# Pooled attention and top-1 experts on one core: two of eight folds keep three chunks, the token numbers are cast by ScalarE, and the order is made anew

## The chip, the core and the metric

The kernel runs on one core of a Trainium2 chip. TensorE (PE) multiplies, VectorE (DVE), ScalarE (ACT) and GpSimd (POOL) work on elements, SyncE (SP) issues most DMAs; each engine works through a queue of its own, in a fixed order, and waits on semaphores. The metric is the time of one execution in microseconds of the device.

## The reference

For 8 batches, 8 heads, 1152 positions and head size 64: queries are averaged in pairs (576 pooled queries), then softmax attention over all 1152 keys. Its output, as 4608 tokens of 512 features, goes through a layer of 8 experts of which each token takes the best one.

```python
q_pool = q.reshape(B, H, S // 2, 2, D).mean(axis=3)
scores = np.matmul(q_pool, k.transpose(0, 1, 3, 2)) / np.sqrt(D)
attn = np.exp(scores - scores.max(-1, keepdims=True))
attn = attn / (attn.sum(-1, keepdims=True) + 1e-09)
x = np.matmul(attn, v)                       # then as (4608, 512)
logits = x @ w_gate
expert_idx = np.argmax(logits, axis=1)       # gate_w: softmax value of it
for e in range(E):
    mask = expert_idx == e
    out[mask] = gate_w[mask, None] * (np.maximum(x[mask] @ w1[e], 0.0) @ w2[e])
```

## The kernel before

Attention goes batch by batch, pair of heads by pair (four), and half of the queries by half (288 columns): a unit. A unit's scores come in nine chunks of 128 keys. For each chunk TensorE makes the scores of both heads in four tiles of 64 x 64 (L592) into one of two banks `st`, and VectorE takes them to SBUF as `s` while it keeps a running minimum (L597). The minimum of all chunks goes over TensorE (L615) and VectorE (L621) to `bias`; ScalarE takes exponentials of three chunks at a time (L625); TensorE multiplies them with the values (L696), and ScalarE and VectorE add the two halves of that into `xT` (L701, L702). Four units may be in flight (`s` has four buffers).

The sums of the exponentials: POOL folds the nine chunks of a unit to one in three adds (L671 to L674): chunks 0 to 2 plus 3 to 5, plus 6 to 8, and then, of the three chunks that are left, the third onto the first. TensorE sums what is left over the partitions, in four tiles of 32 columns (L680). So `total` reads chunk 0 and chunk 1 of `fold`. The last three pairs of the last batch are not folded: TensorE sums all nine chunks (L666).

Keys and pooled queries are transposed by TensorE in two pieces for each pair (L537, L543) and copied out by ScalarE to `kT` and `qT` (L549, L559): one piece with key chunk 8 and the queries, one with key chunks 0 to 7. POOL makes the pooled queries (L496).

At the end of a batch comes its routing. The sums are turned and inverted to `rec` (L711 to L724). TensorE makes the logits (L771), ScalarE copies them (L792), TensorE turns them (L778), and VectorE works out the expert, the gate and the place of each token in its expert's list (L784 to L838): `weight` holds the cast of the token numbers `tok` to integers (L824), `count` adds 576 to `tok` for the next batch (L838). ScalarE copies `rec` in twelve small pieces (L854), VectorE transposes rows (L859), SP writes them to DRAM, and POOL writes the lists with six indirect DMAs (L875).

The experts follow: POOL gathers rows by indirect DMA (L976), ScalarE and VectorE split tokens and weights in a high and a low part (L1144, L1161, L1099), TensorE multiplies three times for each product (L1193, L1224, L1254), POOL scatters the results (L1262).

The order is not written out by hand. A planner (class `Flow`, method `emit`) takes steps with an engine, an expected duration, a key, predecessors and buffers, and works through a plan in which each free engine takes the ready step with the lowest key whose buffers are free. Constants named K_... set the keys of load, transposes, maximum, exponentials, folds, values and routing against their unit; KEEP says how far in key TensorE may stay in one tiling. What comes out is the fixed order of every engine's queue. Buffers and semaphores follow from that order.

Of the kernel before, what the change touches and what calls it, by code (L numbers as in the profile page):

```python
# [12 lines left out]
I32 = mybir.dt.int32  # L13
# [12 lines left out]
COLS, QUADS, ROWS = 1, 2, 3  # L26
# [1 line left out]
FOLD_BUFS = 2  # L28
ROW_BUFS = 3
PAIR = 40  # L30
K_LOAD = -57
K_V = -36
K_POOL = -7
K_PIECE = -26
K_TOP = -17
K_MAX = -18
K_EXP = 13
K_SUM = 25
K_AV = 51
K_ROW = 47  # L40
K_ROUTE = 55
K_CHAIN = 0
K_FIRST = 37
K_PUT = 88
K_SPREAD = 4
K_NEXT = 41
TABLE_OPS = 3
REST = (32, 64)
K_TAB = 0
K_SLOT = 45  # L50
SLOT = 100
RAW = 6
XT = 2
LI_BUFS = 6
RE_BUFS = 8
LEAD = 100
AHEAD = 270
XR2 = 4
XR = 7
Y_BUFS = 3  # L60
DMA = 2000
KEEP = 21
LAST = 3
EXPS = 3
FILL = 3
# [3 lines left out]
CALM, CALM_X = 700, 500  # L69
# [23 lines left out]
class Flow:  # L93
# [8 lines left out]
    def add(self, eng, ns, fn, key=0.0, after=(), holds=(), tiled=False, late=0, paced=0):  # L102
        if self.room is None:
            fn()
            return None
        for h in holds:
            h.left += 1
        step = [key, len(self.steps), eng, ns, fn, list(holds), 0, [], True, list(after), tiled, late, paced]
        for a in after:
            a[7].append(step)  # L110
            step[6] += 1
        self.steps.append(step)
        return step
# [154 lines left out]
def kernel(  # L268
# [10 lines left out]
    nc = tc.nc  # L279

    B, H, S, D = q.shape
# [5 lines left out]
    NJ = NQ // QP  # L287
    HQ = NQ // 2
    NC = S // P
    NHP = H // 2  # L290
# [3 lines left out]
    NQD = P // BL  # L294
# [32 lines left out]
    ones4 = const.tile([P, NHP, 2, 32], F32, name="ones4")  # L327
# [62 lines left out]
    tok = const.tile([QP, NJ], F32, name="tok")  # L390
# [25 lines left out]
    class Pools:  # L416
        h = None
# [29 lines left out]
    def pool(n):  # L447
        return 138 + 2.137 * n
# [14 lines left out]
    def done(*steps):  # L463
        return [s for s in steps if s is not None]
# [190 lines left out]
    def chunk_sum(o, f, key, s, ready, b, hp, half, sums, last):  # L655


        key += K_SUM
        if not o.exact and b == B - 1 and hp >= NHP - LAST:

            def whole():
                for i in range(0, NC, 2):
                    for j in range(min(2, NC - i)):
                        for h in range(2):
                            to = slice(64 * j + 32 * h, 64 * j + 32 * h + 32)
                            nc.tensor.matmul(sums.t[to, :HQ], ones4[:, hp, half, :], s.t[:, i + j, h], start=False,  # L666
                                             stop=hp == NHP - 1 and half == 1 and i + j + 2 >= NC, tile_position=(0, to.start))

            return f.add("PE", 485 * (NC + 1) // 2, whole, key + 10, [*every(ready), *done(*last)], [s, sums], COLS)
        u = tile_of(o, "fold", [P, 3, 2, HQ], bufs=FOLD_BUFS, pool=o.rt)  # L670
        add = lambda to, a, b: nc.gpsimd.tensor_tensor(to, a, b, ALU.add)  # L671
        p = f.add("POOL", pool(6 * HQ), lambda: add(u.t, s.t[:, 0:3], s.t[:, 3:6]), key, every(ready[:6]), [s, u])
        p = f.add("POOL", pool(6 * HQ), lambda: add(u.t, u.t, s.t[:, 6:9]), key, done(p, *every(ready[6:])), [s, u])
        p = f.add("POOL", pool(2 * HQ), lambda: add(u.t[:, 0], u.t[:, 0], u.t[:, 2]), key, done(p), [u])  # L674

        def total():
            for i in range(2):
                for h in range(2):
                    to = slice(64 * i + 32 * h, 64 * i + 32 * h + 32)
                    nc.tensor.matmul(sums.t[to, :HQ], ones4[:, hp, half, :], u.t[:, i, h], start=hp == half == 0,  # L680
                                     stop=hp == NHP - 1 and half == 1, tile_position=(0, to.start))

        return f.add("PE", 500, total, key + 15, done(p, *last), [u, sums], COLS)

    def values(o, f, key, x, s, ready, hp, half, xT):
        pa = [bank(o), bank(o)]
# [55 lines left out]
    def routing(o, f, key, b, xT, rec, sums, ready, hold=()):  # L742
# [5 lines left out]
        lw, ex, de = (tile_of(o, n, s, bufs=1) for n, s in (  # L748
            ("lw", [QP, NJ, H, NE]), ("ex", [QP, NJ, NE]), ("de", [QP, NJ, NE])))
        mx, fm, gate = (tile_of(o, n, [QP, NJ], bufs=1) for n in ("lmx", "fm", "gate"))  # L750
        ohb = tile_of(o, "ohb", [QP, NJ, NE], BF16, bufs=1)
        di = tile_of(o, "di", [QP, NJ], I32, bufs=one)
        re = tile_of(o, "re", [QP, NJ, 2], bufs=one)
        chain = [lw, ex, de]
        key -= (b == B - 1) * 20
        at = key + K_ROUTE
# [34 lines left out]
        p = f.add("PE", 1050, logits, at, ready, [pl, xT], COLS)  # L791
        p = f.add("ACT", act(HQ) - 44, lambda: nc.scalar.copy(lg.t, pl.t[:, :HQ]), at, done(p), [pl, lg])  # L792
        p = f.add("PE", 330, turn, at, done(p), [pt, lg])
# [25 lines left out]
        def weight():  # L819

            nc.vector.tensor_reduce(sum_(), ex.t, axis=AX.X, op=ALU.add)
            nc.vector.tensor_scalar(gate.t, sum_(), 1e-9, None, op0=ALU.add)

            nc.vector.tensor_copy(re.t.bitcast(I32)[:, :, 0], tok)  # L824
            nc.vector.reciprocal(re.t[:, :, 1], gate.t)

        def places():
# [11 lines left out]

        gap = K_CHAIN if b is not None and b < B - 2 else 0  # L840
        p = f.add("DVE", 1100, best, at + 2 + gap, done(*weighed), [*chain, pt])
        e = f.add("ACT", 230, lambda: nc.scalar.activation(ex.t, ex.t, AF.Exp), at + 2 + gap, done(p), [ex])
        p = f.add("DVE", 920, first, at + 2 + 2 * gap, done(p), [pt, ohb])
        r = f.add("PE", 360, rank, at + 3 + 2 * gap, done(p), [pr, ohb])
        w = f.add("DVE", 640, weight, at + 3 + 3 * gap, done(p, e), [ex, re, pt])
        p = f.add("DVE", 670, places, at + 3 + 4 * gap, done(r, w), [pr, pt, de, di])
        c = f.add("DVE", 400, count, at + 4 + 5 * gap, done(p), [pt, lw, ex, de])

        def put(g):

            row = tile_of(o, "row", [P, NJ, RUN], bufs=ROW_BUFS)

            def spread(d):
                nc.scalar.copy(row.t[d * BL:(d + 1) * BL, :, P:],  # L854
                               recf()[g * BL:(g + 1) * BL].rearrange("p j (a s) -> p j a s", s=2)[:, :, :, d * BL // D])

            def turn(j0):
                cols = xT.t.rearrange("p a (j g i) -> p j g a i", j=NJ, g=NB)
                nc.vector.transpose(row.t[:, j0:j0 + NR, :P].rearrange("p j (a x) -> p j a x", a=NHP), cols[:, j0:j0 + NR, g])  # L859

            def store():
                bq = b if b is not None else o.batch
                first = bq * NQ + g * BL * NJ
                rows = planes[:, first:first + BL * NJ] if isinstance(bq, int) else planes[:, bass.ds(first, BL * NJ)]
                for d in range(NQD):
                    nc.sync.dma_start(out=rows[d].rearrange("(i j) x -> i (j x)", j=NJ),
                                      in_=row.t[d * BL:(d + 1) * BL].rearrange("p j x -> p (j x)"))

            at = key + K_ROUTE + K_PUT * g / NB
            p = [f.add("ACT", 115, lambda d=d: spread(d), at + K_SPREAD, ready, [rec, row]) for d in range(NQD)]  # L870
            p += [f.add("DVE", dve(NR * P), lambda j=j: turn(j), at + K_PUT * j / NJ / NB, ready, [row, xT]) for j in range(0, NJ, NR)]
            return f.carry("SP", 480 * NQD, store, -1000.0, done(*p, *hold), [row], 1900)

        def enlist(j):
            ins = nc.gpsimd.indirect_dma_start(  # L875
                out=lists, out_offset=bass.IndirectOffsetOnAxis(ap=di.t[:, j:j + 1], axis=0),
                in_=re.t[:, j, :], in_offset=None, bounds_check=NE * LIST - 1, oob_is_err=False,
            )
            if b is not None:

                for other in stores:
                    tc.declare_no_dep(ins.ins, other.ins, reason="places in the lists are unique")
                stores.append(ins)
            return ins

        outs = [c]
        for g in range(NB):
            outs.append(put(g))
        for j in range(NJ):
            outs.append(f.carry("POOL", 1230, lambda j=j: enlist(j), at + (K_PUT if b is None or b < B - 2 else 0) * j / NJ, done(p, *hold), [di, re], 40, 4400, paced=CALM))  # L890
        return outs

    def first_slots(o, f, key, ready):
# [383 lines left out]
    with ExitStack() as cm, ExitStack() as units, ExitStack() as pairs:  # L1277
# [14 lines left out]
        hold = []  # L1292
# [8 lines left out]
        for b in range(B):  # L1301
            xT = tile_of(o, "xT", [P, NHP, NQ])
            rec = tile_of(o, "rec", [QP, 2, 3, H])
            sm = tile_of(o, "sm", [P, HQ], bufs=1)
            outs, sums, summed = [], sum_bank(o), []
# [6 lines left out]
            key = PAIR * (b * NHP + NHP)  # L1312
            outs.append(row_sums(o, f, key, sums, done(*summed), rec, sm, b == B - 1))
            outs = routing(o, f, key, b, xT, rec, sums, [*outs, router], hold)
            if b == B - 2:
                hold, first = first_slots(o, f, key + K_FIRST, outs)
# [9 lines left out]
        at = key + K_SLOT  # L1326
        for i, ns in enumerate(((EARLY_N,),) * EARLY + RANKS):
            s = i if i < EARLY else i - EARLY
            w, experts = Pools(), (early if i < EARLY else ranked)[:, 0]
# [20 lines left out]
    with tc.If(some > 0):  # L1350
        again = nc.values_load(stab[0:1, 1:2], min_val=0, max_val=1,
                               skip_runtime_bounds_check_because="a comparison's result")
        with tc.If(again > 0):
            reset_state()
            empty_lists()
            with ExitStack() as cm:
                o = open_attention(True, cm, cm, cm)
                with tc.For_i(0, B, 1) as b:
                    f = Flow()
                    xT = tile_of(o, "xT", [P, NHP, NQ])  # L1360
                    rec = tile_of(o, "rec", [QP, 2, 3, H])
# [52 lines left out]
```

## Time and profile before

| | us |
|---|---|
| median of 3 runs (1199.91 to 1202.28) | 1201.47 |
| the profiled execution | 1202.09 |
| its span | 1200.5 |
| TensorE busy | 1163.5 |
| POOL busy | 851.3 |
| VectorE busy | 785.4 |
| ScalarE busy | 636.6 |

The span runs from the first instruction to the end of the last. Attention ends at about 744 us, the experts fill the rest. The logits of the batches start at 121.26, 211.72, 298.80, 388.44, 480.05, 571.42, 660.68 and 750.34 us, and a stretch from one to the next is called a batch here. TensorE's granted clock is at its higher level, 2.4 GHz, in nearly the whole span (mean 0.995 of it). A busy TensorE is not one at its peak: products in different tiles overlap, so their pace is read from start to start.

### The profile page before, as it was taken

The numbers are of one execution on the slowest core, as the hardware profiler recorded it, in microseconds if no ns is written. First come the engines' busy times: TensorE is split into PE (matmuls) and PEld (weight loads), VectorE is DVE, ScalarE is ACT, GpSimd is POOL, SyncE is SP. The second block draws the span as 40 slices with busy tenths as digits, with TensorE's granted clock in tenths as the row PEclk, the third lists the DMA queues.
The fourth block names the chain that finished last, engine by engine and source line by source line (L and its number), as shares of the span: only waits on it lengthen the run. The fifth ranks groups of instructions, "written<-read, shape, count | busy, mean of one in ns | idle before, by whom it ended". The sixth has DMA issues, their size and how long they took to land.

```text
span 1200.5 us, 34022 instructions
## 1 busy us (share of the span) xinstructions
PE 1163.5 (97%) x14199; PEld 819.5 (68%) x14199; DVE 785.4 (65%) x2149; ACT 636.6 (53%) x786; POOL 851.3 (71%) x469
## 2 busy tenths in 40 slices
PE   8999999999999999999999999999999999999996
PEld 4555565555565455465556555898898989999985
DVE  5767867867867866876867965885454644536440
ACT  4666666666666566566666546443342433525440
POOL 2999899899899899899999625355666665541010
PEclk9999999999999999999999999999999999999999
DMA  6653435424624424635425432584353434525320
GB/s 178 147 147 94 109 64 138 108 65 111 134 63 121 100 70 112 128 68 131 111 68 133 89 121 86 139 240 135 93 162 89 154 118 128 152 89 186 120 84 20
DMA packets 78050, 138.12 MB, mean 115 GB/s; under 512 B 11321, under 2 KB 35777, under 8 KB 77888
## 3 DMA queue, kind: packets, MB, share of 16 engines
q1 hardware_dynamic: 68176, 116.22, 37.0%
q0 software_dynamic: 9712, 19.64, 5.6%
q8 instruction: 113, 1.85, 0.7%
q14 instruction: 49, 0.40, 0.1%
HBM read 115.04 MB, written 21.02 MB: 113 GB/s over the span
## 4 chain that ended last, share of the span: by engine, by line
PE 46%; issue 4%; POOL 3%; DVE 3%; ACT 2%; DMA 1%; POOLq 0%; DVEq 0%; ACTq 0%
PE ph L1193 16%; PE py L1254 11%; PE m L696 6%; PE st L592 5%; PE py L1224 5%; POOL fold L671 2%; PE sums L666 1%; DVE s L597 1%; ACT s L625 1%; PE sums L680 1%; DMA qn<-in_q_dram 1%; PE m L1243 0%; POOL xr L976 0%; POOL qp L496 0%; DVE row L859 0%
## 5 line engine op out<-in xcount | busy, mean ns | idle before, releaser
L597 DVE TENSOR_SCALAR_CACHE_REDUCE s<-st 128x576 f32<-128x576 f32 x576 | 419.5, 753 | 158.4 <-PE st L592 152.6
L625 ACT ACTIVATE s<-s,bias 128x1728 f32<-128x1728 f32 x192 | 320.5, 1729 | 166.8 <-DVE bias L621 151.9
L592 PE MATMUL st<-qT,kT 64*64 64x288 f32 x4608 | 364.3, 410 | 10.5 <-DVE s L597 8.6
L696 PE MATMUL m<-s,vn 64*64 64x288 f32 x4608 | 356.5, 405 | 0.0
L592 PEld LDWEIGHTS st<-qT,kT 64*64 64x64 f32 x4608 | 160.2, 132 | 150.3 <-DVE s L597 61.6
L696 PEld LDWEIGHTS m<-s,vn 64*64 64x64 f32 x4608 | 176.1, 133 | 85.9 <-issue 3.5
L671 POOL TENSOR_TENSOR fold<-fold,s 128x1728 f32<-128x1728 f32 x58 | 224.6, 3873 | 1.3
L671 POOL TENSOR_TENSOR fold<-s 128x1728 f32<-128x1728 f32 x58 | 224.3, 3868 | 1.2 <-ACT s L625 1.1
L976 POOL DMA_INDIRECT xr<-x_runs,ix x99 | 109.4, 1105 | 86.3 <-DMA raw<-in_moe_w_dram 20.7
L1193 PE MATMUL ph<-xh,w1h 128*128 128x384 f32 (+6 forms) x480 | 151.4, 315 | 4.0 <-ACT xh L1144 3.0
L1193 PE MATMUL ph<-xl,w1h 128*128 128x384 f32 (+6 forms) x480 | 149.7, 312 | 0.3 <-DVE xl L1099 0.3
L1193 PE MATMUL ph<-xh,w1l 128*128 128x384 f32 (+6 forms) x480 | 149.2, 311 | 0.0
L1262 POOL DMA_INDIRECT out_dram<-y,rec x41 | 45.6, 1112 | 143.0 <-ACT hh L1200 49.7
L1202 DVE SCALAR_TENSOR_TENSOR hl<-ph,hh 128x384 fp32r<-128x384 f32 (+5 forms) x100 | 54.9, 550 | 96.9 <-ACT hh L1200 82.6
L1200 ACT ACTIVATE hh<-ph 128x384 fp32r<-128x384 f32 (+5 forms) x100 | 48.7, 487 | 128.6 <-PE ph L1193 115.1
L1193 PEld LDWEIGHTS ph<-xh,w1h 128*128 128x128 f32 x480 | 91.2, 190 | 7.5 <-ACT xh L1144 3.5
L1193 PEld LDWEIGHTS ph<-xl,w1h 128*128 128x128 f32 x480 | 91.1, 190 | 1.6 <-DVE xl L1099 1.0
L1193 PEld LDWEIGHTS ph<-xh,w1l 128*128 128x128 f32 x480 | 90.9, 189 | 0.0
L1254 PE MATMUL py<-w2h,hh 128*128 128x512 f32 x224 | 88.6, 395 | 0.0
L1254 PE MATMUL py<-w2h,hl 128*128 128x512 f32 x224 | 88.3, 394 | 0.0
L1254 PE MATMUL py<-w2l,hh 128*128 128x512 f32 x224 | 88.0, 393 | 0.0
L875 POOL DMA_INDIRECT lists<-re,di x48 | 46.2, 963 | 55.9 <-PE m L696 21.4
(188 smaller groups left out, 1474.1 us busy)
## 6 DMA issues: line engine op xcount, KB each, us to landing
raw<-in_moe_w_dram SPq DMA_DIRECT2D x80, 512.0 KB
qn<-in_q_dram SPq DMA_DIRECT2D x62, 384.0 KB
vn<-in_v_dram SPq DMA_DIRECT2D x32, 576.0 KB
kn<-in_k_dram SPq DMA_DIRECT2D x31, 576.0 KB
x_runs<-row SPq DMA_DIRECT2D x96, 99.0 KB
xr<-x_runs,ix POOLq DMA_INDIRECT x99
x_runs<-empty SPq DMA_DIRECT2D x4, 297.0 KB
xq<-x_runs,ix POOLq DMA_INDIRECT x49
```

The lines of the kernel that those rows point to most:

```text
L592: made = nc.tensor.matmul(pt.t[to, h, :HQ], x.kT.t[up, c * P + i * D:c * P + (i + 1) * D], x.qT.t[up, cols], start=True, stop=True, tile_p ...
L597: nc.vector.tensor_scalar(s.t[:, c], pt.t[:, :, :HQ], -SCALE, None, op0=ALU.mult, op1=ALU.min, accum_out=mx.t[:, c:c + 1],)
L625: nc.scalar.activation(s.t[:, c0:c0 + n], s.t[:, c0:c0 + n], AF.Exp, bias=bias.t, scale=-1.0)
L671: add = lambda to, a, b: nc.gpsimd.tensor_tensor(to, a, b, ALU.add)
L696: made = nc.tensor.matmul(pa[i].t[cs, :HQ], x.vn.t[up, h, c, :], s.t[up, c, h], start=c == 0, stop=c == NC - 1, tile_position=(up.start, c ...
L875: ins = nc.gpsimd.indirect_dma_start(out=lists, out_offset=bass.IndirectOffsetOnAxis(ap=di.t[:, j:j + 1], axis=0), in_=re.t[:, j, :], in_o ...
L976: return nc.gpsimd.indirect_dma_start(out=x.xr[i // NQD].t[:, i % NQD, :], out_offset=None, in_=xg, in_offset=bass.IndirectOffsetOnAxis(ap ...
L1193: made = nc.tensor.matmul(view()[:, i, :], a[:, c, fp], b[:, c, :n], start=c == 0 and k == 0, stop=c == NDC - 1 and k == 2)
L1200: a = f.add("ACT", act(nb * n) - 44, lambda fs=fs, view=view: nc.scalar.activation(hidden(m)[0][:, fs, :n], view(), AF.Relu), at - 20, don ...
L1202: d = f.add("DVE", dve(nb * n), lambda fs=fs, view=view: nc.vector.scalar_tensor_tensor(hidden(m)[1][:, fs, :n], view(), 0.0, hidden(m)[0] ...
L1224: made = nc.tensor.matmul(py.t[:, :n], a[:, c % 2, ds], b[:, c, :n], start=c == 0 and k == 0, stop=c == NFC - 1 and k == 2)
L1254: made = nc.tensor.matmul(py.t[:n], a[:, c, hs], b[:, c % 2, :], start=c == 0 and k == 0, stop=c == NFC - 1 and k == 2)
```

## The change

Four things change. In the second half of every odd pair the third add is left out; TensorE sums the third chunk itself, two halves of 144 columns for two heads, in the four tiles. The cast of the token numbers moves from VectorE to ScalarE, as a step of its own that is ready when the routing begins; the writes of the lists and the add to `tok` wait for it. The planner expects 225 instead of 115 ns for each of the small copies of `rec` (and other figures for the steps above). And nearly all constants of the planner have other values, so the order of all engines is another from the first pair on.

```diff
-K_V = -36
-K_POOL = -7
-K_PIECE = -26
+K_V = -26
+K_POOL = -1
+K_PIECE = -12
...
-KEEP = 21
+KEEP = 12
...
-        p = f.add("POOL", pool(2 * HQ), lambda: add(u.t[:, 0], u.t[:, 0], u.t[:, 2]), key, done(p), [u])
+        three = hp % 2 and half
+        if not three:
+            p = f.add("POOL", pool(2 * HQ), lambda: add(u.t[:, 0], u.t[:, 0], u.t[:, 2]), key, done(p), [u])
...
+            for i in range(2 if three else 0):
+                for h in range(2):
+                    to = slice(64 * i + 32 * h, 64 * i + 32 * h + 32)
+                    w = slice(i * HQ // 2, (i + 1) * HQ // 2)
+                    nc.tensor.matmul(sums.t[to, w], ones4[:, hp, half, :], u.t[:, 2, h, w], start=False,
+                                     stop=last, tile_position=(0, to.start))
+
+        return f.add("PE", 750 if three else 500, total, key + 15, done(p, *last), [u, sums], COLS)
...
-            nc.vector.tensor_copy(re.t.bitcast(I32)[:, :, 0], tok)
...
-        w = f.add("DVE", 640, weight, at + 3 + 3 * gap, done(p, e), [ex, re, pt])
+        i = f.add("ACT", 200, lambda: nc.scalar.copy(re.t.bitcast(I32)[:, :, 0], tok), at, done(*ready), [re])
+        w = f.add("DVE", 460, weight, at + 3 + 3 * gap, done(p, e), [ex, re, pt])
...
-        c = f.add("DVE", 400, count, at + 4 + 5 * gap, done(p), [pt, lw, ex, de])
+        c = f.add("DVE", 400, count, at + 4 + 5 * gap, done(p, i), [pt, lw, ex, de])
...
-            p = [f.add("ACT", 115, lambda d=d: spread(d), at + K_SPREAD, ready, [rec, row]) for d in range(NQD)]
+            p = [f.add("ACT", 225, lambda d=d: spread(d), at + K_SPREAD, ready, [rec, row]) for d in range(NQD)]
```

How the queues change is seen in three places (numbers in names tell buffers apart; lines of the changed kernel are 9 higher behind the new products). TensorE before, in the second batch: values, three score products in a row, values, one score product, a fold's sums, transposed keys.

```order
L696 MATMUL m_1990<-s_1639,vn_1306 64x288 x2
L696 MATMUL m_1993<-s_1639,vn_1306 64x288 x2
L592 MATMUL st_2093<-qT_1780,kT_1778 64x288 x4
L592 MATMUL st_2099<-qT_1780,kT_1778 64x288 x4
L592 MATMUL st_2107<-qT_1780,kT_1778 64x288 x4
L696 MATMUL m_2114<-s_1877,vn_1306 64x288 x2
L696 MATMUL m_2117<-s_1877,vn_1306 64x288 x2
L592 MATMUL st_2122<-qT_1780,kT_1778 64x288 x4
L680 MATMUL sums_1943<-fold_1973,ones_73 32x288 x4
L537 MATMUL st_2134<-ident,kp_1806 128x64 x2
```

TensorE now, in the same batch, around a fold of three chunks.

```order
L705 MATMUL m_2107<-s_1823,vn_1312 64x288 x2
L705 MATMUL m_2110<-s_1823,vn_1312 64x288 x2
L592 MATMUL st_2219<-qT_1969,kT_1967 64x288 x4
L592 MATMUL st_2227<-qT_1969,kT_1967 64x288 x4
L705 MATMUL m_2235<-s_2023,vn_1605 64x288 x2
L705 MATMUL m_2238<-s_2023,vn_1605 64x288 x2
L683 MATMUL sums_1935<-fold_2125,ones_73 32x288 x4
L689 MATMUL sums_1935<-fold_2125,ones_73 32x144 x4
L537 MATMUL st_2251<-ident,kp_2005 128x64 x16
L537 MATMUL st_2275<-ident,kp_2005 128x64 x2
```

Scores come in pairs, the four products of the third chunk stand right behind the fold's sums, and both pieces of transposed keys follow one another. VectorE before, in the second batch's routing: the expert's place, weights with the cast, takes of scores.

```order
L807 CAST ohb_3104<-sums_1943 96x48
L621 TENSOR_REDUCE bias<-st_3106 128x1
L821 TENSOR_REDUCE sums_1943<-ex_3068 96x6
L822 TENSOR_SCALAR gate<-sums_1943 96x6
L824 CAST re_3124<-tok 96x6
L825 RECIPROCAL re_3124<-gate 96x6
L597 TENSOR_SCALAR s_3089,mx<-st_3070 128x576
L597 TENSOR_SCALAR s_3089,mx<-st_3128 128x576
```

VectorE now, in the same routing.

```order
L816 CAST ohb_3077<-sums_1935 96x48
L621 TENSOR_REDUCE bias<-st_3079 128x1
L597 TENSOR_SCALAR s_3062,mx<-st_3065 128x576
L830 TENSOR_REDUCE sums_1935<-ex_3036 96x6
L831 TENSOR_SCALAR gate<-sums_1935 96x6
L833 RECIPROCAL re_2885<-gate 96x6
L597 TENSOR_SCALAR s_3062,mx<-st_3096 128x576
```

The cast is gone from this queue and a take of scores stands between the steps. The cast now stands in ScalarE's queue, in the routing of the fifth batch as in the others, among the copies of `rec` and ahead of the copy of the logits.

```order
L863 COPY row_6592<-rec_6574 32x6x4 x4
L853 CAST re_6608<-tok 96x6
L863 COPY row_6615<-rec_6574 32x6x4 x4
L502 COPY kp_6633<-kn_6333 128x2x9x64
L863 COPY row_6654<-rec_6574 32x6x4 x4
L801 COPY sm_6673<-sums_5659 128x288
```

Before, an exponential and four to twelve of these copies stand from the first copy of `rec` to that of the logits, and no cast.

## Rows read from the trace of the kernel before

**Rows 1.** Page, busy time by engine, share of span, instructions
```profile
PE 1163.5 (97%) x14199; PEld 819.5 (68%) x14199; DVE 785.4 (65%) x2149; ACT 636.6 (53%) x786; POOL 851.3 (71%) x469
```

**Rows 2.** Window table by stage: us, busy us of each engine, clock, DMA share, GB/s
```profile
0.00:50.00 50.00, 43.68 (x592) 23.33 (x596) 32.53 (x157) 24.93 (x27) 27.60 (x23) 1.00 0.58 157
50.00:744.00 694.00, 678.96 (x11024) 391.08 (x11017) 510.46 (x1527) 434.02 (x470) 613.36 (x258) 1.00 0.43 103
744.00:825.00 81.00, 76.89 (x384) 66.17 (x385) 61.69 (x159) 38.63 (x66) 42.62 (x39) 0.96 0.60 169
825.00:1200.50 375.50, 363.99 (x2206) 338.92 (x2204) 180.69 (x307) 139.01 (x225) 167.71 (x152) 0.99 0.39 119
```

**Rows 3.** Window table, sum over batches two to seven
```profile
sum 539.42, PE 527.30 PEld 305.09 DVE 399.95 ACT 341.94 POOL 506.29; mean PE 87.88 PEld 50.85 DVE 66.66 ACT 56.99 POOL 84.38
```

**Rows 4.** Who TensorE waited for: us in total, times, longest
```profile
PE st L592 <- DVE s L597: 8.6, 21, 1.4
PE sums L680 <- POOL fold L671: 3.7, 8, 1.4
PE sums L778 <- ACT sm L792: 3.3, 4, 1.0
PE st L592 <- ACT kT L549: 1.2, 5, 0.5
```

**Rows 5.** Groups by form: count, busy us, mean ns, idle; L824 min/median/max ns
```profile
L671 POOL TENSOR_TENSOR fold<-s 128x1728 f32<-128x1728 f32 x58 | 224.3, 3868 | 1.2 <-ACT s L625 1.1
L671 POOL TENSOR_TENSOR fold<-fold 128x576 f32<-128x576 f32 x58 | 81.9, 1413 | 0.8
L625 ACT ACTIVATE s<-s,bias 128x1728 f32<-128x1728 f32 x192 | 320.5, 1729 | 166.8 <-DVE bias L621 151.9 <-DVE s L597 8.1 <-DVE xr L1136 4.3
L549 ACT COPY kT<-st 128x1024 f32<-128x1024 f32 x31 | 31.5, 1015 | 24.8 <-PE st L537 23.5 <-PE st L592 1.3
L559 ACT COPY qT<-st 128x576 f32<-128x576 f32 x31 | 20.0, 646 | 0.0
L549 ACT COPY kT<-st 128x128 f32<-128x128 f32 x31 | 8.2, 264 | 37.8 <-PE st L543 37.6 <-issue 0.2
L824 DVE CAST re<-tok x8: 157/564/1789, 131.3 to 764.3; 96x6 int32<-96x6 f32 x8
```

**Rows 6.** Timeline, TensorE at 148 us: start, us, operation, idle before
```profile
148.74 0.71 PE L592 MATMUL st<-qT,kT 64*64 64x288 f32 x8 [0.41 <-DVE s L597]
149.27 0.66 PE L696 MATMUL m<-s,vn 64*64 64x288 f32 x8
149.76 0.66 PE L592 MATMUL st<-qT,kT 64*64 64x288 f32 x8
150.35 0.69 PE L680 MATMUL sums<-fold,ones 128*32 128x288 f32 x8
150.97 0.28 PE L537 MATMUL st<-ident,kp 64*128 64x64 f32 x2
```

**Rows 7.** Timeline behind two casts: TensorE, POOL, VectorE
```profile
400.41 0.72 PE L592 MATMUL st<-qT,kT 64*64 64x288 f32 x8 [1.16 <-DVE s L597]
...
489.17 1.84 POOL L496 TENSOR_TENSOR qp<-qn 128x768 f32<-128x768 f32 x1
489.38 1.66 DVE L824 CAST re<-tok 96x6 int32<-96x6 f32 x1
491.92 1.20 PE L592 MATMUL st<-qT,kT 64*64 64x288 f32 x16 [1.42 <-DVE s L597]
```

**Rows 8.** Timeline where the first expert begins: ScalarE, TensorE
```profile
745.16 1.99 ACT L1161 CAST w1h<-raw 128x1024 fp32r<-128x1024 f32 x2
747.72 0.69 PE L1193 MATMUL ph<-xh,w1h 128*128 128x384 f32 x1 [1.73 <-ACT xh L1144]
```

**Rows 9.** Adds to tok (L838): min/median/max ns; POOL behind one
```profile
L838 DVE TENSOR_SCALAR tok<-tok x7: 159/160/164, 133.8 to 673.0; 96x6 f32<-96x6 f32 x7
493.92 0.92 POOL L875 DMA_INDIRECT lists<-re,di  x1 [2.90 <-PE m L696]
```

More of the change, by code (lines that the diff above doesn't have):

```diff
@@ L30 @@
 PAIR = 40
-K_LOAD = -57
-K_V = -36
-K_POOL = -7
-K_PIECE = -26
[L35 to L40, printed above, removed]
-K_ROUTE = 55
[L42 to L46, printed above, removed]
+K_LOAD = -63
+K_V = -26
+K_POOL = -1
+K_PIECE = -12
+K_TOP = -16
+K_MAX = -26
+K_EXP = 21
+K_SUM = 26
+K_AV = 50
+K_ROW = 66
+K_ROUTE = 55
+K_CHAIN = 6
+K_FIRST = 20
+K_PUT = 89
+K_SPREAD = -27
+K_NEXT = 28
 TABLE_OPS = 3
 REST = (32, 64)
-K_TAB = 0
-K_SLOT = 45
+K_TAB = -1
+K_SLOT = 53
 SLOT = 100
@@ L55 @@
 RE_BUFS = 8
-LEAD = 100
-AHEAD = 270
+LEAD = 123
+AHEAD = 227
 XR2 = 4
@@ L673, in chunk_sum @@
         p = f.add("POOL", pool(6 * HQ), lambda: add(u.t, u.t, s.t[:, 6:9]), key, done(p, *every(ready[6:])), [s, u])
-        p = f.add("POOL", pool(2 * HQ), lambda: add(u.t[:, 0], u.t[:, 0], u.t[:, 2]), key, done(p), [u])
+        three = hp % 2 and half
+        if not three:
+            p = f.add("POOL", pool(2 * HQ), lambda: add(u.t[:, 0], u.t[:, 0], u.t[:, 2]), key, done(p), [u])
         def total():
+            last = hp == NHP - 1 and half == 1
             for i in range(2):
@@ L680, in total @@
                     nc.tensor.matmul(sums.t[to, :HQ], ones4[:, hp, half, :], u.t[:, i, h], start=hp == half == 0,
-                                     stop=hp == NHP - 1 and half == 1, tile_position=(0, to.start))
-        return f.add("PE", 500, total, key + 15, done(p, *last), [u, sums], COLS)
+                                     stop=last and not three, tile_position=(0, to.start))
+            for i in range(2 if three else 0):
[5 more added lines that the diff above has]
+        return f.add("PE", 750 if three else 500, total, key + 15, done(p, *last), [u, sums], COLS)
     def values(o, f, key, x, s, ready, hp, half, xT):
@@ L889, in routing @@
         for j in range(NJ):
-            outs.append(f.carry("POOL", 1230, lambda j=j: enlist(j), at + (K_PUT if b is None or b < B - 2 else 0) * j / NJ, done(p, *hold), [di, re], 40, 4400, paced=CALM))
+            outs.append(f.carry("POOL", 1230, lambda j=j: enlist(j), at + (K_PUT if b is None or b < B - 2 else 0) * j / NJ, done(p, i, *hold), [di, re], 40, 4400, paced=CALM))
         return outs
```

## Prediction

> **What bounds the kernel now.** I read the busy line of the page first, then the span cut into stages, then one table over six whole batches, then who TensorE waited for, and last the timeline at the waits that came out largest. TensorE is busy for 97% of the span [rows 1]. By stages [rows 2] it idles 6.3 us in the opening (50.00 less 43.68), 15.0 us in the rest of attention (694.00 less 678.96), 4.1 us where the first experts begin and 11.5 us from 825 us on, nearly all of it after the last matmul. So a change to attention and to its end can win back about 15 + 4 us of plain idle time, no more, besides work that it saves TensorE.
>
> GpSimd (POOL) is the second engine at its limit: over six batches of 89.9 us each (539.42 / 6) it is busy 506.29 of 539.42 us, TensorE 527.30 [rows 3]. But TensorE waited for a fold only 3.7 us in all, eight times; it waited 8.6 us, 21 times, for VectorE to free a score bank [rows 4]. TensorE therefore sets the pace and POOL runs close behind it. A microsecond saved on POOL is worth only what TensorE waited for it.
>
> **The change part by part.**
>
> *The third chunk.* Of eight folds in a batch two keep three chunks. In batches one to seven that is 14 folds; the last three pairs of the last batch are not folded at all, before or after. POOL loses 14 adds of 1413 ns [rows 5], 19.8 us. TensorE gains 14 sets of four tile products of 144 columns. The trace has no such shape; the nearest row is the same sum over 288 columns. It starts at 150.35 and the transposes behind it at 150.97 [rows 6], 0.62 us, of which 0.10 is the change of tiling: score and value sets follow each other at 0.49 us (149.27 to 149.76), and before the sums it is 0.59 (149.76 to 150.35). That leaves 0.52 us for 288 columns. If cost goes with columns a new set takes 0.26 us, 14 x 0.26 = +3.6 us; if a set costs the same however short, 14 x 0.52 = +7.3 us. The set stands right behind the existing four, in the same tiling, so no further change of tiling is paid. I take +3.6, as columns set the pace of that row.
>
> *What POOL's relief is worth.* At most the 3.7 us of fold waits, at least nothing. The relief is 2.8 us a batch, but only two of eight folds get shorter themselves. I take half, -1.8.
>
> *The cast.* On VectorE eight casts of 96 x 6 numbers took 157 ns at best and 1789 at worst [rows 5]. The one at 489.38 ran until 491.04, and POOL's add that began at 489.17 ended at 491.01 [rows 7]: the cast stood still until POOL was done. TensorE's next score product then came 1.42 us late, at 491.92; behind the longest cast, of 1789 ns, TensorE waited 1.16 us at 400.41 [rows 7]. On ScalarE a copy of 128 x 128 takes 264 ns [rows 5], and the cast hardly more, hidden by an engine busy 434 of 694 us [rows 2]. I take -2.6; without a cover, if ScalarE's copies run late, it is 0. The Trainium skill ("SBUF — State Buffer", section "SBUF: two separate sides") says that a VectorE instruction that uses the port pair shared with GpSimd waits until the other's whole instruction is over, and that ScalarE never waits so. The trace agrees at 489.38. The rule has a second side, which is a rival below.
>
> *The new order.* Rows of the order up to the first expert: changes of tiling on TensorE fall from 251 to 234. 17 x 0.10 = -1.7 us. Scores use two banks and VectorE starts a new take every 0.67 us or so, so a third score product in a row waits: 0.41 us at 148.74 [rows 6]. Third and later ones in a row fall from 21 to 13; the seven in batches two to seven all go. 8 x 0.41 = -3.3 us (0 if the pairs left wait in their place). The wait of the logits' transpose for ScalarE's copy, 3.3 us in four places [rows 4], may vanish or double: 0, with both ends kept. In the order of the changed kernel two score products (0.97 us) stand there in nearly every batch, but ScalarE now has the cast, a key copy and up to twelve row copies in its queue ahead of that copy.
>
> Against this, transposed keys now come just in time. Before, most pieces with eight key chunks lie several microseconds ahead of the first score that reads them; now, in batches two to seven, three to five sets, 1.45 to 2.4 us. The copies behind both pieces of a pair take 264 + 646 + 1015 ns [rows 5], 1.9 us. If ScalarE is free this just fits; if an exponential (1729 ns) [rows 5] is in front, it doesn't. TensorE's waits for these copies so far: 1.2 us in five, 0.24 each [rows 4]. For six such pieces of work, one a batch, I take +1.5; below nothing it can't go by more than the 1.2; the upper end is under the rivals.
>
> *Start of the experts.* TensorE waits 1.73 us at 747.72 for the first expert's tokens (xh). ScalarE made two weight casts, 1.99 us, right before that copy [rows 8]; in the new order there is one. -1.0 (bounds 0 and -1.7). From the third expert on the order of the matmuls is the old one, and I count nothing there.
>
> Sum: +3.6 - 1.8 - 2.6 - 1.7 - 3.3 + 1.5 - 1.0 = -5.3 us. The profiled execution took 1202.09 us (span 1200.5 and 1.6 around it), 0.6 above the median of 1201.47. 1202.1 - 5.3 - 0.6 = 1196 us.
>
> **Rivals.**
>
> *POOL was the real bound (about 1187).* For it: POOL is idle almost only before its list writes, and a batch of 89.9 us is little above POOL's 84.4 and these gaps. Then 14 x 1.41 = 19.8 us less on POOL shortens attention until TensorE binds: all 15.0 us idle in attention goes, and 3.6 come back, with 1.7 and 1.0 from tiling and start: -14. Against it: 3.7 us of waits for folds.
>
> *Nothing on balance (1199 to 1204).* The new sets cost 7.3 instead of 3.6, or pairs of scores wait where the triples did (+3.3): -5.3 + 3.7 or + 3.3 gives about 1200. For it: a VectorE that is busy 510 of 694 us frees banks no sooner than before.
>
> *Keys too late (about 1206, slower).* Place: the first score product of a pair in each of 24 pairs (batches two to seven). It decides when the exponential ahead in ScalarE's queue ends later than the transposes: the copies then end up to 1.7 us later, the slack is 0.5 us, and each pair waits up to 1.2. At half of that in two of three pairs, 16 x 0.6 = 10 us: 1196 + 10 = 1206. Against it: the order puts ScalarE's copy of the pair before (L701) between exponentials and key copies, so the exponentials are meant to be over.
>
> *The wait moves to the add of 576 (about 1203, slower).* The running token number stays on VectorE, one input and one output in SBUF as the cast has. Its seven instances took 160 ns, but in each POOL stood idle: it was waiting for its first list write, as in the 2.90 us before the one at 493.92 [rows 9]. With a shorter chain on VectorE and a POOL that no longer waits, the add can fall into a fold of 3.87 us [rows 5]: half of that, 1.9 us, of which TensorE felt some 1.3 at the two casts; in six batches 6 x 1.3 = 7.8, on 1196 some 1204. The Trainium skill's rule ("SBUF — State Buffer", same section) speaks for it. The trace speaks neither way, since no add met a busy POOL.
>
> **How the numbers follow.** A run of this kernel can tell a change of 0.2%, 2.4 us, from none. Forecast case, 2.4 to 10 us faster: 0.52. POOL the bound, more than 10 faster: 0.11. Nothing on balance: 0.18. Keys too late: 0.12. Add that waits: 0.07. So faster 0.63, same 0.18, slower 0.19. Range: the POOL case as lower end, 1187, the late keys as upper end, 1206; the likeliest case alone spans 1191 to 1199.
>
> **What would show it.** Right: the fold waits under L680 shrink; the cast is gone from VectorE and no gap over 1 us stands in front of a score product in the routing; idle before score products for VectorE falls by some 3 us; a new set takes about 0.26 us; the wait at the first expert halves. Wrong: waits of score products for ScalarE's key copies above 5 us; an add to tok of more than 0.5 us; logits' transposes that wait 1 us in each batch; TensorE's idle time in attention still at 15 us.

## The result and the profile after

The changed kernel takes 1183.4 us (median; 1182.2 to 1184.3), the kernel before took 1201.3 beside it: a ratio of 0.9848, 95% interval 0.9834 to 0.9863. About 5 us were predicted and 18 came. In what follows times are set against the kernel before on the same chip, since that one took between 1194 and 1202 us on the chips that were drawn; 0.1% is 1.2 us. The changed kernel itself came out at 0.9848, 0.9855 and 0.9881 in three sets of runs, so ratios from different sets can be compared to some 0.3%, 4 us, and no closer.

The page of the profile after, busy time by engine; it answers to [rows 1]:

```profile
PE 1156.3 (98%) x14311; PEld 831.9 (70%) x14311; DVE 780.4 (66%) x2141; ACT 638.9 (54%) x794; POOL 831.4 (70%) x455
```

The window table after, cut as in [rows 2], but with the first matmul of the experts 16.6 us earlier (731.14 after 747.72) and the end 19.9 earlier; columns as there:

```profile
0.00:50.00 50.00, 44.42 (x624) 24.13 (x628) 33.25 (x158) 26.30 (x28) 31.01 (x25) 1.00 0.61 168
50.00:727.40 677.40, 672.82 (x11094) 404.29 (x11090) 503.86 (x1520) 436.53 (x476) 592.92 (x242) 1.00 0.40 105
727.40:806.00 78.60, 75.89 (x404) 65.76 (x397) 62.50 (x159) 36.75 (x65) 40.75 (x38) 1.00 0.59 178
806.00:1180.60 374.60, 363.15 (x2200) 337.76 (x2198) 180.80 (x307) 139.34 (x226) 166.70 (x151) 0.99 0.39 120
```

TensorE's idle time in attention fell from 15.0 us to 4.6 (677.40 less 672.82), at the start of the experts from 4.1 to 2.7; opening and end are nearly as they were. In all it idles 12.7 us less (37.0 to 24.3) and is busy 7.2 us less, although it has 14 sets of four products more (112 in the page, which counts each of these products twice). That it is busy for less time because of fewer changes of tiling and of waits too short to show as idle time is how I read it, and not tried.

The same table over batches two to seven, from logits to logits, which answers to [rows 3]:

```profile
sum 527.21, PE 523.92 PEld 317.73 DVE 395.50 ACT 346.28 POOL 493.01; mean PE 87.32 PEld 52.95 DVE 65.92 ACT 57.71 POOL 82.17
```

A batch takes 87.9 us instead of 89.9. TensorE idles 0.55 us in it instead of 2.0.

Who TensorE waited for after, against [rows 4] (us in total, times, longest):

```profile
PE st L592 <- DVE s L597: 4.5, 14, 0.5
...
PE st L592 <- ACT qT L559: 0.8, 2, 0.6
...
PE ph L1202 <- ACT xh L1153: 0.8, 1, 0.8
PE sums L787 <- ACT sm L801: 0.7, 1, 0.7
```

The score products' waits for VectorE fell from 8.6 to 4.5 us and the longest from 1.4 to 0.5; the waits for folds, 3.7 before, are gone, and those of the logits' transposes for ScalarE's copy fell from 3.3 to 0.7. Behind these lines the code is the old one; the sums stand at L683 and L689 now, and what follows eight or nine lines further down.

The adds of GpSimd and the cast after, against [rows 5] (the first row a group of all lines, the second one line's instructions with min, median and max in ns):

```profile
L671 POOL TENSOR_TENSOR fold<-fold 128x576 f32<-128x576 f32 x44 | 62.3, 1416 | 1.1
...
L853 ACT CAST re<-tok x8: 195/196/198, 112.5 to 735.9; 96x6 int32<-96x6 f32 x8
```

There are 14 third adds fewer, 19.6 us, and a cast that takes 0.2 us on ScalarE every time.

### The profile page after: what moved, and what is told of

It is laid out like the page before. It is cut to its first block, busy times and chain, and to the rows that moved or that the text cites. A ratio compares the mean times of both kernels' runs of the same rounds, so it can differ in the third digit from the quotient of the medians.

```text
span 1180.6 us, 34250 instructions
## 1 busy us (share of the span) xinstructions
PE 1156.3 (98%) x14311; PEld 831.9 (70%) x14311; DVE 780.4 (66%) x2141; ACT 638.9 (54%) x794; POOL 831.4 (70%) x455
## 5 line engine op out<-in xcount | busy, mean ns | idle before, releaser
L597 DVE TENSOR_SCALAR_CACHE_REDUCE s<-st 128x576 f32<-128x576 f32 x576 | 420.1, 754 | 135.8 <-PE st L592 125.3
L592 PEld LDWEIGHTS st<-qT,kT 64*64 64x64 f32 x4608 | 167.1, 132 | 132.7 <-DVE s L597 50.1
L705 PEld LDWEIGHTS m<-s,vn 64*64 64x64 f32 x4608 | 181.7, 133 | 83.8 <-issue 2.6
```

The lines of the kernel that those rows point to most:

```text
L592: made = nc.tensor.matmul(pt.t[to, h, :HQ], x.kT.t[up, c * P + i * D:c * P + (i + 1) * D], x.qT.t[up, cols], start=True, stop=True, tile_p ...
L597: nc.vector.tensor_scalar(s.t[:, c], pt.t[:, :, :HQ], -SCALE, None, op0=ALU.mult, op1=ALU.min, accum_out=mx.t[:, c:c + 1],)
L705: made = nc.tensor.matmul(pa[i].t[cs, :HQ], x.vn.t[up, h, c, :], s.t[up, c, h], start=c == 0, stop=c == NC - 1, tile_position=(up.start, c ...
```

## The experiments

Theory A, as first written down: GpSimd's load held TensorE late, so the two edits (third chunk, cast) bring the gain by themselves. Theory B: the new order brings it. Theory C: neither does without the other, because the new order is cut to the shorter folds (the fold is GpSimd's adds for one unit, the sum TensorE's product that takes it). In all but the last two kernels (code_only and const_only) the order of each engine is kept as it is in its parent, row for row, except for the instructions that are edited.

**The edits on the old order, and the new order without the edits**

In the old order, third chunk (old_chunk), cast (old_cast) and both (old_both):

```
-  ... lambda: add(u.t[:, 0], u.t[:, 0], u.t[:, 2]) ...
+  ... lambda: None if three else add(u.t[:, 0], u.t[:, 0], u.t[:, 2]) ...   # three = hp % 2 and half
+  (total() as in the changed kernel, with the products of 144 columns)
-  nc.vector.tensor_copy(re.t.bitcast(I32)[:, :, 0], tok)                    # in weight()
+  nc.scalar.copy(re.t.bitcast(I32)[:, :, 0], tok)                           # behind ScalarE's copy of the logits
```

In the new order both taken back (new_alone):

```
-  lambda: add(u.t, u.t, s.t[:, 6:9])
+  lambda: (add(u.t, u.t, s.t[:, 6:9]), three and add(u.t[:, 0], u.t[:, 0], u.t[:, 2]))
   (no products of 144 columns; the cast in weight(), on VectorE)
```

> The old order, with one edit: in the same 14 folds the third chunk is summed by TensorE in four tile products of 144 columns, and GpSimd's third add is left out; the output is the whole reference's. Theory A (GpSimd's load held TensorE late, so the edits themselves bring the gain): 14 x 1.41 = 19.8 us less on GpSimd, the waits on folds go to nearly 0 and the score and value waits that follow from them shrink: 1190 to 1195. Theory B (the new order brings it): only the 3.7 us of fold waits can go and 14 x 0.22 = 3.1 us of new products come: 1199 to 1202. Theory C (both are needed, since the order was made for the lighter GpSimd): as B.

> The old order, with one edit: the cast of the token numbers is issued by ScalarE right behind its copy of the logits, VectorE's is gone. VectorE's eight casts took 6.0 us in all, and TensorE felt 1.42 and 1.16 us of two of them. Theory A: 1196 to 1199, as the stalls of the casts also push later score products back. Theories B and C: about 1199 to 1201, the 2.6 us at most.

> The old order with both edits, third chunk and cast. Theory A: 1184 to 1190, most of the 18 us. Theory B: 1197 to 1201. Theory C: 1197 to 1201 as well; the fourth run of this set tells B from C.

> The new order, with both edits undone: GpSimd makes the third add in all folds, straight behind the second add, TensorE has no products of 144 columns, VectorE makes the cast within the same step as before. Theory A: 1196 to 1203, TensorE waits for folds again (over 5 us) and behind the casts. Theory B: 1181 to 1188, as the new products' 3.1 us go and the waits do not come back. Theory C: 1190 to 1200, since the order has no room for the adds that it does not plan for.

Measured: 1.0000 (0.9991 to 1.0009), 0.9997 (0.9988 to 1.0006), 0.9999 (0.9990 to 1.0008) and 1.0057 (1.0043 to 1.0072). A falls by the first three, B by the last: the edits alone bring nothing, the order alone costs 0.57%, 6.8 us. Only C stands, with its guess of 1190 to 1200 for new_alone a little too low (1200.8, which lies in A's 1196 to 1203). TensorE's waits in new_alone are those that the sums then have for the third adds:

```profile
PE sums L683 <- POOL fold L671: 14.4, 13, 1.3
```

Beside a trace of before on the same chip, once more:

> The kernel before once more, for its trace on the chip of this set. Every theory: ratio 1.000.

> The old order with both edits once more, beside a trace of before on the same chip. Theory C (the edits pay only in an order that is made for them): ratio 0.998 to 1.001, as at first, with waits for folds of about 3 us left. If this chip has long casts in before (6 us on VectorE in eight), the cast's share could show as up to 5 us: 0.995 to 1.000.

Measured: 1.0008 (0.9998 to 1.0019) and 0.9996 (0.9986 to 1.0006). Where GpSimd's relief went is in its own waits, here between 120 and 660 us: first before, then with both edits in the old order.

```profile
POOL lists L875 <- PE m L696: 20.0, 19, 3.5
POOL lists L875 <- PE st L592: 4.4, 4, 2.2
POOL lists L875 <- DVE tok L838: 2.1, 1, 2.1
```

```profile
POOL lists L882 <- DVE s L597: 14.3, 5, 3.9
POOL lists L882 <- ACT s L625: 11.4, 6, 4.1
POOL lists L882 <- PE st L592: 7.1, 5, 3.2
POOL lists L882 <- PE m L704: 7.0, 10, 2.0
POOL fold L671 <- ACT s L625: 4.2, 4, 1.6
```

The busy time of GpSimd fell by 16.7 us in this stretch (507.61 to 490.96), and the same time came back as waits: before list writes 42 us instead of 31 (the idle column of their group: 30.9 and 42.1), before folds 4. A list write is held until TensorE has come to the write's place in the order (the program adds that wait to every paced step), so a GpSimd that is early there stands until TensorE arrives. The profile puts 25.7 of the 42 us down to VectorE and ScalarE; that they go with this wait too is seen further down, in old_free, where it is 7.2 us.

TensorE itself has no use for a fold that is ready sooner, for the old order places the sums of these 14 folds late. One of them in old_both_2, the second add and the sums:

```profile
372.02 3.86 POOL L671 TENSOR_TENSOR fold<-fold,s 128x1728 f32<-128x1728 f32 x1
...
379.33 0.69 PE L682 MATMUL sums<-fold,ones 128*32 128x288 f32 x8
```

The add ends at 375.88 and the sums start 3.45 us later, where before there was room for the third add. Over the 14 folds this gap is 2.1 to 5.8 us in old_both_2. In the first trace of before TensorE waited at two of these 14 sums only, 1.7 of its 3.7 us; its other waits, and the 2.3 us that stay in old_both_2, are at folds that keep their third add. What did fall in the old order is the wait of score products for VectorE, 8.2 us in before_2 and 5.6 in old_both_2, and no time came of it that these runs can tell.

**One edit at a time in the new order**

new_chunk takes only the third chunk back, new_cast only the cast, by the lines above; the changed kernel and the kernel before ran beside them.

> The changed kernel once more, beside the other runs of this set, so that they can be set against it on the same chip. Every theory: 0.985 of the time of before, as at first.

> The kernel before once more, for a trace of it on the chip of this set: ratio 1.000. If the waits of score products for VectorE (8.6 us in the first trace of before, 5.0 to 5.5 in the three edited ones in the old order) come out near 5 us here, that difference was the chip's and not the edits'.

> The new order with only the chunk edit undone: GpSimd makes the third add in all folds, straight behind the second add, and TensorE has no products of 144 columns; the cast stays on ScalarE. Theory C (the new order puts the sums of these 14 folds where only a fold without a third add is over): TensorE waits at 13 or 14 sums for about 1.1 us each, 14 to 15 us, less the 3.1 us of products: 11 to 12 us slower than the changed kernel, and hardly any other wait moves. If GpSimd's load were what binds (theory A), the whole difference to the run with both edits undone, some 25 us, shows here.

> The new order with only the cast edit undone: VectorE makes it in the same step as before. Theory C (what remains of the 25 us between the two new-order kernels belongs to the cast): 8 to 13 us slower than the changed kernel, with score products late by over 1 us behind most casts. A rival: the cast is worth what its own stalls are, 3.4 us on VectorE in all, of which TensorE feels at most half: 0 to 2 us slower, and the rest of the 25 us comes from both edits undone together, since a GpSimd that runs late meets the casts more often.

Measured: 0.9855 (0.9838 to 0.9872), 1.0002 (0.9991 to 1.0013), 0.9975 (0.9962 to 0.9987), 0.9914 (0.9900 to 0.9929). So in the new order the third chunk is worth 0.0120, 14.4 us (11 to 12 were expected), and the cast 0.0059, 7.1 us; together 21.5, close to what lies between new_alone and the changed kernel (1.0057 less 0.9855, 24 us, across two chips). The waits of score products for VectorE are as long in this trace of before (8.3 us) as in the first and in before_2 (8.2), so the shorter ones of the edited kernels in the old order (5.0 to 5.6) came with the edits and are not shown to be their chip's.

Who TensorE waited for in new_chunk:

```profile
PE sums L683 <- POOL fold L671: 13.1, 13, 1.3
PE st L592 <- DVE s L597: 4.4, 14, 0.5
PE st L543 <- POOL qp L496: 2.3, 6, 0.4
```

One place of it on the timeline (start, length, operation, idle time in front), GpSimd and then TensorE:

```profile
331.55 3.88 POOL L671 TENSOR_TENSOR fold<-fold,s 128x1728 f32<-128x1728 f32 x1
335.51 1.40 POOL L671 TENSOR_TENSOR fold<-fold 128x576 f32<-128x576 f32 x1
336.87 1.81 POOL L496 TENSOR_TENSOR qp<-qn 128x768 f32<-128x768 f32 x1
...
336.96 0.69 PE L683 MATMUL sums<-fold,ones 128*32 128x288 f32 x8 [1.33 <-POOL fold L671]
337.59 0.77 PE L537 MATMUL st<-ident,kp 64*128 64x64 f32 x18
338.74 0.46 PE L543 MATMUL st<-ident,qp 48*128 48x48 f32 x8 [0.38 <-POOL qp L496]
```

The same place in the changed kernel (after_again):

```profile
326.29 3.87 POOL L671 TENSOR_TENSOR fold<-fold,s 128x1728 f32<-128x1728 f32 x1
330.11 1.81 POOL L496 TENSOR_TENSOR qp<-qn 128x768 f32<-128x768 f32 x1
...
330.31 0.69 PE L683 MATMUL sums<-fold,ones 128*32 128x288 f32 x8
330.81 0.43 PE L689 MATMUL sums<-fold,ones 128*32 128x144 f32 x8
331.17 0.77 PE L537 MATMUL st<-ident,kp 64*128 64x64 f32 x18
331.97 0.58 PE L543 MATMUL st<-ident,qp 48*128 48x48 f32 x12
```

This is the heart of it. The second add ends at 330.16 and the sums start at 330.31, 0.15 us later; the query repacking behind it ends at 331.92 and the query transposes start at 331.97. The new order has TensorE take both things almost as soon as GpSimd has made them. In the changed kernel's trace the gap between second add and sums is 0.13 to 0.14 us for six of the 14 folds, 0.47 to 0.53 for six, and 0.66 and 1.46 for the two of the first batch; in the old order it was 2.1 us and more. Put the third add of 1.40 us back, and TensorE stands 1.33 us at the sums and 0.38 at the queries here, and 13.1 us in 13 such places for the sums alone.

In new_cast the waits of score products for VectorE are 10.5 us instead of 4.5, again in 14 places, the longest 1.7. One of them:

```profile
303.81 1.41 POOL L671 TENSOR_TENSOR fold<-fold 128x576 f32<-128x576 f32 x1
...
303.89 1.35 DVE L833 CAST re<-tok 96x6 int32<-96x6 f32 x1
305.16 0.18 DVE L834 RECIPROCAL re<-gate 96x6 f32<-96x6 f32 x1
305.26 0.71 DVE L597 TENSOR_SCALAR_CACHE_REDUCE s<-st 128x576 f32<-128x576 f32 x1
...
306.12 0.71 PE L592 MATMUL st<-qT,kT 64*64 64x288 f32 x8 [1.71 <-DVE s L597]
```

The cast begins 0.08 us behind an add of GpSimd and ends with it (305.24 and 305.22); in this order the batches are nearly alike, and the cast is held so in six of eight (four times for 1.35 us, once for 1.25, once for 0.81). My guess of 8 to 13 us was a little high, the rival's 0 to 2 wrong.

**Is it the fold's length or GpSimd's load?**

new_load keeps both edits, but has GpSimd make an add of the same size behind the second one, whose result nobody reads; new_four drops the third add in 15 more folds.

```
-  lambda: add(u.t, u.t, s.t[:, 6:9])
+  lambda: (add(u.t[:, :3], u.t[:, :3], s.t[:, 6:9]), three and add(u.t[:, 3], u.t[:, 0], u.t[:, 2]))   # new_load; u has a fourth chunk
-  three = hp % 2 and half
+  three = half                                                                                         # new_four, same order
```

> The new order with both edits, but GpSimd makes an add of the same 128 x 576 behind the second add of the same 14 folds, whose result nobody reads: GpSimd's load is that of before again, 19.8 us more, while the sums need only the two adds. Theory C (the sums of these folds wait for the fold's own length, not for GpSimd's load): within 3 us of the changed kernel, ratio about 0.986 to 0.988, no wait on the 14 sums. Theory A (the load binds): near the run with the third add back, 0.9975.

> The new order, unchanged, with the third add dropped in four folds of eight instead of two (15 more), and their third chunk summed by TensorE: 15 x 1.41 = 21.2 us less on GpSimd, 15 x 0.22 = 3.3 us more on TensorE. Theory C: no sum waits for a fold any more, so only TensorE's 3.3 us count: ratio 0.9855 + 0.0027 = 0.988. Theory A: faster again, 0.975 to 0.983.

Measured: 0.9965 (0.9953 to 0.9978) and 0.9870 (0.9855 to 0.9886). new_load went against theory C as I had put it: no sum waits, and yet most of the third chunk's gain is gone; the ratio is closer to theory A's 0.9975 than to C's 0.986 to 0.988. TensorE's waits in it, and one place:

```profile
PE st L543 <- POOL qp L496: 9.2, 6, 1.5
PE st L592 <- DVE s L597: 4.5, 14, 0.5
```

```profile
333.26 1.41 POOL L671 TENSOR_TENSOR fold<-fold 128x576 f32<-128x576 f32 x1
334.63 1.80 POOL L496 TENSOR_TENSOR qp<-qn 128x768 f32<-128x768 f32 x1
...
333.32 0.69 PE L683 MATMUL sums<-fold,ones 128*32 128x288 f32 x8
333.83 0.43 PE L689 MATMUL sums<-fold,ones 128*32 128x144 f32 x8
334.19 0.77 PE L537 MATMUL st<-ident,kp 64*128 64x64 f32 x18
336.48 0.59 PE L543 MATMUL st<-ident,qp 48*128 48x48 f32 x12 [1.52 <-POOL qp L496]
```

The sums start in time, and the repacking of the next pair's queries, next in GpSimd's queue, is 1.5 us late, once a batch. It is thus neither the load as a total nor the fold's own length: it is every piece of GpSimd's queue that TensorE takes without slack. new_four shows the other side: with 21 us less on GpSimd nothing more is won (theory A had 0.975 to 0.983). What the 15 new sets of products cost, 3.3 us expected, cannot be told: 0.9870 lies within the changed kernel's own 0.9848 to 0.9881.

**The hold of the list writes**

```
-  if s[12] and self.pe is not None:
+  if s[12] and s[3] != 1230 and self.pe is not None:      # list writes wait for their data alone
```

> The old order with both edits, and list writes on GpSimd that no longer wait for their place in TensorE's order (they still wait for their data). If that hold eats the relief (19.8 us less work came back as 11 us more idle time before list writes and 4 us before folds): 0.990 to 0.997 of before. If the old order's sums and score products wait for other things: 0.999 to 1.001 as with the hold.

> The changed kernel without that hold of the list writes, nothing else changed. GpSimd waits there 28 us in six batches, but TensorE waits for no fold: 0.984 to 0.987, no difference to the changed kernel (0.9855). If the hold also keeps GpSimd late where TensorE feels it by way of VectorE's copies: 0.980 to 0.984. If free list writes collide with other transfers: above 0.988.

Measured: 0.9968 (0.9956 to 0.9981) and 0.9873 (0.9856 to 0.9890). Against old_both (0.9999) the hold seems to have eaten about 0.3%, 3.7 us, of what the edits could bring in the old order. That compares two chips, and is as much as the changed kernel differs between sets; the traces go the same way, with 0.2 us of waits for folds in old_free and 3.0 in old_both. The rest of the 21 us that the edits are worth in the new order was not to be had there by this means: between 120 and 660 us GpSimd now waits 18.7 us before list writes instead of 42.1, but 19.6 instead of 4.3 before the first adds of folds, mostly for exponentials. For the new order the changed kernel had to run beside it:

> The changed kernel beside the one without the hold, on one chip: 0.985 to 0.988 of before.

> The changed kernel without the hold of the list writes. If the new order does not pay for the hold: within 0.1% of the changed kernel. If it does: 0.1 to 0.4% faster, as the old order with both edits was (0.9968 against 0.9998).

Measured: 0.9881 (0.9864 to 0.9897) and 0.9870 (0.9854 to 0.9887). No difference that can be told: this version does not beat the changed kernel.

**What makes the new order: the planner's knowledge or its constants?**

code_only is the changed code with the constants of before, const_only the code of before with the new constants; both are planned anew.

> The changed kernel's code with the constants of before: the planner knows of the two folds of three chunks and of the cast on ScalarE, and makes its order by the old numbers. If it is the planner's knowledge that counts: 0.985 to 0.992. If it is the constants (where sums, keys, row copies and routing are due): 0.996 to 1.003.

> The code of before with the new constants: the planner knows that all folds have a third add, so sums are planned behind it, unlike in the run of the new order with both edits undone (1.0057). If the constants alone bring gain: 0.988 to 0.995. If they pay only together with the edits: 0.997 to 1.006.

Measured: 0.9941 (0.9927 to 0.9955) and 1.0219 (1.0203 to 1.0236). Edits that the planner knows of are worth 7 us by the old constants, where the same edits in the old order brought nothing; the new constants on the old code cost 26. With the edits known, the new constants bring another 7 to 11 us (0.9941 against 0.9848 to 0.9881). code_only lies between the two forecasts, const_only outside both. Which of the constants counts most was not tried. In const_only TensorE waits 16.0 us for score banks, up to 3.6 at once:

```profile
PE st L592 <- DVE s L597: 16.0, 37, 3.6
```

## Why the prediction was wrong

*The step that failed: what POOL's relief is worth.* The prediction wrote "At most the 3.7 us of fold waits, at least nothing" and took 1.8. Those waits belong to the old order. In it the bound holds: third chunk, relief and cast were summed to +3.6 - 1.8 - 2.6 = -0.8 us, and both edits measured -0.1 and -0.5 us (0.9999 and 0.9996), with 3.0 and 2.3 us of fold waits left. In the new order the third chunk is worth 14.4 us with its products paid (new_chunk), where +3.6 - 1.8 had it cost 1.8; the relief alone is then some 17.6 us (14.4 and 14 x 0.23 for the products, an estimate), nearly five times the bound. That is because the new order has TensorE at the sums 0.13 to 0.53 us behind the second add in 12 of the 14 folds, where the old one, with the third add gone, has 2.1 us or more. The prediction took the wait that the old order showed for the most that GpSimd's relief could be worth in any order.

*The new order was priced by counting.* Fewer changes of tiling, fewer third score products in a row, later keys, an earlier start: -1.7 - 3.3 + 1.5 - 1.0 = -4.5 us. The new order without the edits measured +6.8. The counts were right in themselves: in the trace after, third and later score products in a row number 13 instead of 21, and TensorE changes its tiling 17 times less. What was left out is where the order puts the sums and the query transposes against GpSimd's queue. Adding the terms of the edits and of the order was the error: -0.5 at most and +6.8 measured apart, -18 together.

*The third chunk's price, +3.6, was right.* In the changed kernel a set of sums with its products lasts from 330.31 to 331.17, 0.86 us; in new_chunk the sums alone last from 336.96 to 337.59, 0.63. That is 0.23 us for a new set, 0.26 predicted.

*The cast, -2.6:* its mechanism was right, its size not. In the old order the cast alone brought 0.4 us (0.9997, not to be told from nothing), although score products waited 5.0 us for VectorE in old_cast and 8.2 to 8.6 in the traces of before. In the new order it is 7.1 us, as six of the eight casts are held by GpSimd, four of them for 1.35 us, with score products behind them.

*Third score products in a row, -3.3; keys just in time, +1.5; logits copy, 0.* The waits for VectorE fell by 4.1 us, which holds this term and the cast's in one (5.9 predicted for both). Of the keys nothing is to be seen: score products waited 1.2 us in five places for kT [rows 4], and after, by the idle column of their group, 0.8 for qT and 0.5 for kT. The logits' copy came out near the good end, 3.3 to 0.7.

*Start of the experts, -1.0, right; behind it 0, wrong.* The wait for xh went from 1.73 us [rows 8] to 0.78. The next one of its kind in the trace of before, which the sum left alone, is also gone:

```profile
822.96 0.44 PE L1193 MATMUL ph<-xh,w1h 128*128 128x384 f32 x1 [1.24 <-ACT xh L1144]
823.69 0.44 PE L1193 MATMUL ph<-xl,w1h 128*128 128x384 f32 x1 [0.28 <-DVE xl L1099]
```

From the first expert to the end the changed kernel is 3.3 us shorter (452.8 to 449.5 us).

The signs that the prediction named for being right all came: no fold waits, no gap over 1 us at a score product of the routing, 4.1 us less waiting for VectorE, a new set at 0.23 us, the wait at the first expert halved. They test the terms one by one, and the terms did not add up to the gain.

*The rivals.* POOL as the real bound, 1187, with a chance of 0.11, came nearest, and its picture is half right: attention did lose 10.4 of the 15 us idle. But it took GpSimd's total for the bound, and by the old order's three runs and new_four less of that total brings nothing. Keys too late and nothing on balance are out. The add to tok waited for GpSimd once in seven, for 0.16 us. The six others fell beside GpSimd's list writes, where before GpSimd stood idle, and took 0.16 us each, the first of them wholly within a write:

```profile
L846 DVE TENSOR_SCALAR tok<-tok x7: 159/160/317, 131.2 to 656.1; 96x6 f32<-96x6 f32 x7
...
130.53 1.08 POOL L884 DMA_INDIRECT lists<-re,di  x1 [1.46 <-PE m L705]
131.16 0.16 DVE L846 TENSOR_SCALAR tok<-tok 96x6 f32<-96x6 f32 x1
```

The shorter waits of the logits' copy and of the experts are the order's: in old_both TensorE still waits 3.2 us for the copies and 3.0 for xh, in new_alone not at all and 0.8. Open stays which of the constants bring the gain.

## What to carry to other kernels

Where a change brings edits and a new static order together, price the edits in the new order: follow the busiest side engine's queue through one batch with durations from the trace and see how much slack each thing has that the main engine takes from it. A wait of the old order bounds what an edit is worth in the old order alone. And test such a change by its four corners (old and new order, with and without the edits) before explaining it.

## What the runs showed of the hardware

The cast of 96 x 6 numbers on VectorE that begins while GpSimd adds ends with GpSimd's add, be it one of a fold or that of the pooled queries: at 305.24 beside one that ends at 305.22 in new_cast, as at 491.04 and 491.01 before [rows 7]. The one slow add to tok is a case of the same: it began at 656.13 and ended at 656.45, and GpSimd's add of 1.42 us from 655.00 on ended at 656.42. The Trainium skill ("SBUF — State Buffer", section "SBUF: two separate sides") says that such an instruction, when it comes second to the ports that VectorE shares with GpSimd, waits for the whole of the other's. The trace agrees for GpSimd's adds. At the list writes it shows no such wait: an add to tok that lies wholly within one takes the 0.16 us that it takes alone, once in the trace after (131.16 to 131.32, the write 130.53 to 131.61) and four times in const_only. The rival that the add would wait in every batch did not come, for in six of seven it fell beside such a write. The takes of score banks (L597), which read from PSUM, did not wait either: in new_cast 279 of them lie wholly within an add of a fold and take 0.755 us in the mean, the 297 others 0.752.

A set of four tile products cost about in proportion to its columns: 0.23 us more for one of 144, and 0.50 from the start of one of 288 to the next in the same tiling (330.31 to 330.81 in after_again).
